# A three-stage network on one core: weight decoding in written order, down products three column blocks behind

## The chip, the cores and the metric

One NeuronCore of a Trainium2 chip runs the whole program. The metric is the time of one execution on the device in microseconds (us); lower is better. TensorE is called PE in the views of the profile (its weight loads PEld), VectorE DVE, ScalarE ACT, GpSimd POOL and SyncE SP.

## The reference

Three stages follow one another on 4 sequences of 768 positions and 384 channels (8 heads of 48). All arrays are 32-bit; the weights of the last two stages come in as 64-bit floats, two words for a number.

```python
# 1. linear attention with decay, per batch and head
cur = u * k_t  (outer)  v_t
y_t = r_t @ (state + cur)
state = w * state + k_t (outer) v_t
# 2. gated feed-forward with a convolution over the sequence (384 -> 1024 -> 384)
h = relu(x @ w_in)
c = conv_w[0]*h[t-1] + conv_w[1]*h[t] + conv_w[2]*h[t+1]     # zeros beyond the ends
x = (h * sigmoid(c)) @ w_out
# 3. normalisation and feed-forward with a residual (384 -> 1536 -> 384)
xn = (x - mean) / sqrt(var + 1e-6) * g_ln
out = x + relu(xn @ w_ch1) @ w_ch2
```

## The kernel before

**Blocks and passes.** The 3072 positions are cut into 24 tiles of 128 for the attention and into 8 blocks of 384 (three tiles) for the two feed-forward stages. There are two passes over the blocks. The first (`mixer1`, blocks j = 0 to 7) does the convolution stage and spills its result to DRAM; the attention tiles are computed beside it. The second (`mixer2`) loads a block back, normalises it and does the last stage. The first four attention tiles come before block 0, in the loop `while finished[0] < EARLY - 1`.

**Products in three parts.** A 32-bit product is made of three products of a reduced 32-bit type: every operand is split into a high part and the remainder (`xh` and `xl`, `wih` and `wil`, `gh` and `gl`), and high x high, high x low and low x high are added in PSUM. So one column block f (128 hidden columns) of a block of positions takes nine products upward (`mm3`, into `psm`) and nine downward (`down`, into the three accumulators `acc`).

**A column block of the first pass.** `moe1_up` issues the nine upward products of column f, then the gate of column f - 1 (`gate`: sigmoid on ScalarE, product on VectorE), then relu, scaling (L371, L372, ScalarE) and two taps (L374, VectorE) of column f, then the split of the gated column f - 1 into `gh` (L360, ScalarE) and `gl` (L361, VectorE). The downward products are put into a list by `queue_down` and run by `pump`: with LAG = 2, column f - 2 goes down in the turn of column f. LAG also sets the number of `gh` and `gl` buffers, LAG + 1. After the upward and after the downward products of a turn, `after1` is called: 16 slots to a block. A slot takes one attention step and some decode steps.

**Attention steps.** `attn_tile` is a generator with five parts: transposes of r and k (`prt`, `pkt`) and the diagonal `aT`; state update (`pst`, `sn`, `sbds`) and the next tile's `kk`; products `dps` and masked copies into `aT`; an empty part; output products `yps`, their split into `xh` and `xl`, the loads of tile n + 3, and the copies of the one column that neighbouring blocks share (L320, L321). Block j of the first pass may begin when tile (j + 1) x 3 - (j mod 2) is done (the last one for j = 7), because of that shared column. Block 0 has 14 attention steps in its slots, the others 16.

**Weight decoding.** `wjob` makes a job of every slice of weights: jobs 0 to 2 (first half of w_in, 512 numbers a partition), 3 (w_out), 4 to 6 (second half of w_in), 7 to 9 (w_out), 10 to 15 (w_ch1), 16 to 21 (w_ch2), 768 numbers each where nothing else is said. A job is loaded into one of three `st` buffers. Its steps: absolute value of the high word (L111, ScalarE) and clamp (L112); shift (L114); two steps that put in the low word's bits and the sign (L117, L119) with the high copy (L140, ScalarE); the remainder (L143, for w_ch1 scaled by `g_ln`, L145). Four calls of the generator make a job, as the last step comes in one call with the next job's first. `wdo(n, last)` makes n such calls, up to job `last`, and loads a job ahead; `need(job)` makes as many calls as it takes to end that job.

**What sets the order.** The program text is an order for the planner of the framework: it simulates a time line and sets every engine's instructions in a fixed order, moving what is free to where its simulated engine has room. Steps given to `tc.keep_in_program_order` keep their written place among one another. Before, these were all TensorE instructions, the loads of `st` and `x1b`, and the two reductions of `choose_path`; the decode steps on VectorE and ScalarE were free.

Of the kernel before, what the change touches and what calls it, by code (L numbers as in the profile page):

```python
# [8 lines left out]
F32 = mybir.dt.float32  # L9
# [20 lines left out]
NP = H // 2  # L30
PR = 112
WN = 768
LAG = 2
EARLY = 4
GC = 16
GE = 4
# [7 lines left out]
def body(ctx, tc, r, k, v, w, u, w_in, conv_w, w_out, g_ln, w_ch1, w_ch2, out):  # L44
    nc = tc.nc
# [17 lines left out]
    class InOrder:  # L63


        def matmul(self, *args, **kw):
            return tc.keep_in_program_order(nc.tensor.matmul(*args, **kw))  # L67

        def transpose(self, *args, **kw):
            return tc.keep_in_program_order(nc.tensor.transpose(*args, **kw))  # L70

    pe = InOrder()


    ident = const.tile([128, 128], F32, name="ident")
# [29 lines left out]
    def decode(st, n):  # L105

        words = st[:, 0:2 * n].rearrange("p (n two) -> p n two", two=2)
        lo, hi = words[:, :, 0], words[:, :, 1]
        t = ap.tile([128, WN], F32, tag="wd", name="wdec", bufs=2)[:, 0:n]
        ti = t.bitcast(I32)  # L110
        a_.activation(out=t, in_=hi.bitcast(F32), func=AF.Abs)  # L111
        v_.tensor_scalar(out=t, in0=t, scalar1=W_MIN, scalar2=W_MAX, op0=ALU.max, op1=ALU.min)  # L112
        yield
        v_.tensor_scalar(out=ti, in0=ti, scalar1=5, scalar2=2, op0=ALU.logical_shift_left,  # L114
                         op1=ALU.logical_shift_right)
        yield
        v_.scalar_tensor_tensor(out=ti, in0=lo, scalar=29, in1=ti, op0=ALU.logical_shift_right, op1=ALU.bitwise_or)  # L117
        yield
        v_.scalar_tensor_tensor(out=ti, in0=hi, scalar=-(2 ** 30), in1=ti, op0=ALU.bitwise_and, op1=ALU.bitwise_or)  # L119
        return t  # L120

    wjobs = []
# [1 line left out]
    def wjob(src, n, hi, lo, scale=None):  # L124

        st = []

        def load():
            st.append(io.tile([128, 2 * WN], I32, tag="st", name="st", bufs=3))
            dst = st[0][:, 0:2 * n]  # L130
            if len(src.shape) == 3:
                dst = dst.rearrange("p (a n) -> p a n", a=src.shape[1])
            tc.keep_in_program_order(nc.sync.dma_start(out=dst, in_=src.bitcast(I32)))

        def steps():
            t = yield from decode(st[0], n)
            if len(src.shape) == 3:
                t = t.rearrange("p (a n) -> p a n", a=src.shape[1])
            kw = {} if scale is None else {"scale": gl[:, scale:scale + 1]}
            a_.activation(out=hi, in_=t, func=AF.Copy, **kw)  # L140
            yield
            if scale is None:
                v_.tensor_tensor(out=lo, in0=t, in1=hi.bitcast(F32), op=ALU.subtract)  # L143
            else:
                v_.scalar_tensor_tensor(out=lo, in0=t, scalar=kw["scale"], in1=hi.bitcast(F32),  # L145
                                        op0=ALU.mult, op1=ALU.subtract)
        wjobs.append((load, steps()))
        return len(wjobs) - 1
# [35 lines left out]
    def wdo(count=1, last=None):  # L184

        for _ in range(count):
            while w_done[0] < (len(wjobs) if last is None else last + 1):
                wload(w_done[0] + 2)
                if next(wjobs[w_done[0]][1], "end") != "end":
                    break  # L190
                w_done[0] += 1
# [359 lines left out]
    def tables():  # L551
# [2 lines left out]
        wv = w.rearrange("(p two) d -> two d p", two=2)  # L554
        for q in range(2):
            nc.sync.dma_start(out=wc[64 * q:64 * q + D], in_=wv[q].unsqueeze(2), allow_slow_non_contiguous=True)
        load_tile(0)
        nc.sync.dma_start(out=tku[:, 1], in_=u.unsqueeze(0).to_broadcast([128, H, D]))
        wload(1)
        load_tile(1)  # L560
        wload(2)
# [49 lines left out]
    def conv_weights(cst):  # L611
        t = yield from decode(cst, 3 * NF1)
        v_.tensor_copy(out=cw, in_=t.rearrange("p (k f) -> p k f", k=3))

    def choose_path():

        wr = sp.tile([1, DM], F32, tag="wr", name="wr", bufs=1)
        ok = sp.tile([1, 4], F32, tag="ok", name="ok", bufs=1)
        nc.sync.dma_start(out=wr, in_=w.rearrange("h d -> (h d)").unsqueeze(0))
        tc.keep_in_program_order(v_.tensor_reduce(out=ok[:, 0:1], in_=wr, axis=AX.X, op=ALU.max))  # L620
        tc.keep_in_program_order(v_.tensor_reduce(out=ok[:, 1:2], in_=wr, axis=AX.X, op=ALU.min))
        v_.tensor_scalar(out=ok[:, 2:3], in0=ok[:, 0:1], scalar1=DECAY_MAX, scalar2=None, op0=ALU.is_le)
        v_.tensor_scalar(out=ok[:, 3:4], in0=ok[:, 1:2], scalar1=DECAY_MIN, scalar2=None, op0=ALU.is_ge)
        v_.tensor_tensor(out=ok[:, 0:1], in0=ok[:, 2:3], in1=ok[:, 3:4], op=ALU.mult)
        v_.tensor_scalar(out=general, in0=ok[:, 0:1], scalar1=0.5, scalar2=None, op0=ALU.is_lt)
# [27 lines left out]

    cst = tables()
    decayed_k(0)
    for _ in conv_weights(cst):
        pass
    tau, early = 0, {}
    while finished[0] < EARLY - 1:
        if tau % 3 == 0 and tau // 3 < EARLY:  # L660
            early[tau // 3] = attn_tile(tau // 3)
        for gen in early.values():
            next(gen, None)
        wdo(1 + tau % 2)
        tau += 1
    ahead = [iter(())]
    for j in range(NB):
        slot = [0]
        while finished[0] < min((j + 1) * TT - (j % 2), NT - 1):
            step()  # L670

        def before1(f):
            if f < NF1:
                need(wi_job[f // 4])
            if f >= LAG:
                need(wo_job[min(f - LAG + 1, NF1 - 1)])

        def after1(f):
            if j or f:
                step()  # L680
            slot[0] += 1
            if j == 0:
                wdo(2)
            elif j < NB - 2:
                wdo(slot[0] % 2, c1_job[NF2 - 1])
            else:
                wdo(1, c2_job[4])
            if j == NB - 1:
                if slot[0] == 1:
                    ahead[0] = prefetch(0)  # L690
                elif slot[0] % 4 == 0:
                    next(ahead[0], None)

        mixer1(xT[j], spill(j), before1, after1)
# [3 lines left out]
    for j in range(NB):  # L698
        def before2(f):
            need(c1_job[f])  # L700
            need(c2_job[f])

        def after2(f):
            wdo(2)
            if f == 1 and j + 1 < NB:
                ahead[0] = prefetch(j + 1)
            if f >= 4:
                next(ahead[0], None)

        b, s0 = divmod(j, BPB)  # L710
        x1s, xn = normed.pop(j)
        mixer2(xn, lambda acc, x1s=x1s, b=b, s0=s0: finish(
            acc, x1s, lambda t0: out[b, s0 * T + t0:s0 * T + t0 + 128, :]), before2, after2)
    pump(0)
    flag = nc.values_load(general[0:1, 0:1], min_val=0, max_val=1)
    with tc.If(flag != 0):
# [31 lines left out]
```

## Time and profile before

| | us |
|---|---|
| time, median of 3 runs (707.03 to 709.63) | 708.38 |
| the profiled execution's own time | 709.03 |
| its span, first to last instruction | 707.5 |
| TensorE busy | 650.5 |
| VectorE busy | 434.9 |
| ScalarE busy | 271.4 |
| GpSimd busy | 98.8 |

Busy times overlap between engines and do not add up to the span. Ends of products are modelled, so TensorE that is busy throughout is not TensorE at its peak. Where an engine idles, the views name what ended the wait. The mean granted clock of TensorE over the span was 0.965 of its full 2.4 GHz.

### The profile page before, as it was taken

How to read it: one execution, taken by the hardware profiler on the slowest of the kernel's cores; microseconds unless marked ns; L12 is line 12 of the kernel's file. 1: busy time of each engine (PE TensorE's matmuls, PEld its weight loads, DVE VectorE, ACT ScalarE, POOL GpSimd, SP SyncE). 2: the span in 40 equal slices, each digit the busy share in tenths (PEclk: the TensorE clock that was granted, in tenths of full speed). 3: DMA queues.
4: the chain of work that ended last, by engine and by line, in shares of the span. 5: the costliest groups of instructions: out<-in, count | busy, mean ns of one | idle time of the engine just before them, and what ended most of it. 6: DMA issues, size and time to landing. Idle time of an engine off the chain costs nothing.

```text
span 707.5 us, 12380 instructions
## 1 busy us (share of the span) xinstructions
PE 650.5 (92%) x5100; PEld 615.1 (87%) x5100; DVE 434.9 (61%) x823; ACT 271.4 (38%) x537; POOL 98.8 (14%) x136
## 2 busy tenths in 40 slices
PE   4765888979999999999499999999999999999996
PEld 3655777869998999989498999999999999999996
DVE  5989999988788878797967534224241424242211
ACT  2436546655565655556566321212111111212110
POOL 5341211122113121230100000000000000000000
PEclk9976889999999999999799999999999999999999
DMA  8954452423132232305000302020010202020001
GB/s 147 228 153 112 124 169 68 120 49 92 34 91 45 58 79 45 103 2 198 4 35 1 112 1 67 1 68 1 29 39 1 68 1 68 0 68 1 34 1 38
DMA packets 93841, 45.14 MB, mean 64 GB/s; under 512 B 80337, under 2 KB 89682, under 8 KB 93778
## 3 DMA queue, kind: packets, MB, share of 16 engines
q1 hardware_dynamic: 93778, 44.28, 23.7%
q8 instruction: 42, 0.69, 0.4%
q14 instruction: 21, 0.17, 0.1%
HBM read 34.83 MB, written 9.44 MB: 63 GB/s over the span
## 4 chain that ended last, share of the span: by engine, by line
PE 71%; DVE 18%; DMA 4%; issue 2%; ACT 2%; SPq 2%; POOL 1%; ACTq 0%; DVEq 0%; POOLq 0%
PE acc L67 32%; PE psm L67 31%; DVE c L374 3%; PE yps L67 3%; DMA st<-in_moe_w_ch_dram 2%; PE dps L67 2%; DVE aT L287 2%; DVE wdec L117 2%; DVE wdec L119 1%; DVE wdec L112 1%; DVE gl L361 1%; PE pxt L70 1%; DVE kk L222 1%; DVE c L355 1%; DVE wdec L114 1%
## 5 line engine op out<-in xcount | busy, mean ns | idle before, releaser
L388 DVE SCALAR_TENSOR_TENSOR rl<-psm,rh 128x384 fp32r<-128x384 f32 x96 | 53.4, 556 | 146.8 <-ACT rh L387 146.8
L387 ACT ACTIVATE rh<-psm 128x384 fp32r<-128x384 f32 x96 | 47.3, 493 | 216.5 <-PE psm L67 213.9
L67 PE MATMUL psm<-xnh,c1h 128*128 128x384 f32 x288 | 99.1, 344 | 0.6 <-ACT xnh L331 0.6
L67 PE MATMUL psm<-xnl,c1h 128*128 128x384 f32 x288 | 97.5, 339 | 0.8 <-DVE xnl L332 0.8
L67 PE MATMUL psm<-xnh,c1l 128*128 128x384 f32 x288 | 97.6, 339 | 0.0
L67 PE MATMUL acc<-c2l,rh 128*128 128x384 f32 x288 | 97.1, 337 | 0.0
L67 PE MATMUL acc<-c2h,rl 128*128 128x384 f32 x288 | 97.1, 337 | 0.0
L67 PE MATMUL acc<-c2h,rh 128*128 128x384 f32 x288 | 97.0, 337 | 0.0
L374 DVE SCALAR_TENSOR_TENSOR c<-h,cw,c 128x384 f32<-128x384 f32 x128 | 86.5, 677 | 11.1 <-ACT c L372 10.0
L67 PE MATMUL acc<-woh,gh 128*128 128x384 f32 x192 | 70.5, 367 | 11.6 <-ACT gh L360 11.6
L67 PE MATMUL acc<-woh,gl 128*128 128x384 f32 x192 | 68.4, 356 | 12.5 <-DVE gl L361 12.5
L67 PE MATMUL psm<-xh,wih 128*128 128x386 f32 x192 | 72.3, 377 | 4.9 <-POOL xl L316 4.6
L67 PE MATMUL psm<-xl,wih 128*128 128x386 f32 x192 | 67.8, 353 | 2.4 <-POOL xl L320 2.4
L67 PE MATMUL psm<-xh,wil 128*128 128x386 f32 x192 | 67.0, 349 | 0.0
L67 PE MATMUL acc<-wol,gh 128*128 128x384 f32 x192 | 66.8, 348 | 0.0
L411 POOL TENSOR_TENSOR rs<-rs,nhalf 128x1 f32<-128x1 f32 x24 | 14.4, 615 | 304.3 <-DVE rs L410 304.1
L354 ACT ACTIVATE c<-c 128x384 f32<-128x384 f32 x64 | 33.5, 524 | 59.4 <-DVE c L374 59.4
L67 PEld LDWEIGHTS psm<-xnl,c1h 128*128 128x128 f32 x288 | 54.4, 189 | 1.1 <-DVE xnl L332 1.0
L67 PEld LDWEIGHTS psm<-xnh,c1h 128*128 128x128 f32 x288 | 54.4, 189 | 0.9 <-ACT xnh L331 0.9
L254 POOL TENSOR_TENSOR av<-kk,rvbuf 128x384 f32<-128x384 f32 x24 | 33.4, 1390 | 155.3 <-DVE kk L222 129.2
L67 PEld LDWEIGHTS psm<-xnh,c1l 128*128 128x128 f32 x288 | 54.2, 188 | 0.0
L67 PEld LDWEIGHTS acc<-c2h,rh 128*128 128x128 f32 x288 | 54.1, 188 | 0.0
(108 smaller groups left out, 1175.7 us busy)
## 6 DMA issues: line engine op xcount, KB each, us to landing
st<-in_moe_w_ch_dram SPq DMA_DIRECT2D x12, 768.0 KB, 5.8
rvbuf<-in_r_dram SPq DMA_DIRECT2D x24, 192.0 KB, 3.2
kt<-in_k_dram SPq DMA_DIRECT2D x24, 192.0 KB, 3.2
rvbuf<-in_v_dram SPq DMA_DIRECT2D x24, 192.0 KB, 2.9
x_dram<-x SPq DMA_DIRECT2D x24, 192.0 KB, 2.0
x1b<-x_dram SPq DMA_DIRECT2D x24, 192.0 KB, 2.8
out_dram<-x1b SPq DMA_DIRECT2D x24, 192.0 KB, 1.9
st<-in_moe_w_in_dram SPq DMA_DIRECT2D x6, 512.0 KB, 5.1
```

The source lines that it names most:

```text
L67: return tc.keep_in_program_order(nc.tensor.matmul(*args, **kw))
L70: return tc.keep_in_program_order(nc.tensor.transpose(*args, **kw))
L112: v_.tensor_scalar(out=t, in0=t, scalar1=W_MIN, scalar2=W_MAX, op0=ALU.max, op1=ALU.min)
L114: v_.tensor_scalar(out=ti, in0=ti, scalar1=5, scalar2=2, op0=ALU.logical_shift_left, op1=ALU.logical_shift_right)
L117: v_.scalar_tensor_tensor(out=ti, in0=lo, scalar=29, in1=ti, op0=ALU.logical_shift_right, op1=ALU.bitwise_or)
L254: g_.tensor_tensor(out=av, in0=kk[:, 1, :, 0:D], in1=rt[:, :, 0:D], op=ALU.mult)
L287: v_.copy_predicated(out=aT[:, q], mask=later.bitcast(I32), data=dps[q])
L354: a_.activation(out=st["c"], in_=st["c"], func=AF.Sigmoid)
L374: v_.scalar_tensor_tensor(out=c, in0=h[:, o:o + T], scalar=cw[:, tap, f:f + 1], in1=c, op0=ALU.mult, op1=ALU.add)
L387: a_.activation(out=gh, in_=ps[:, 0:T], func=AF.Relu)
L388: v_.scalar_tensor_tensor(out=gl_, in0=ps[:, 0:T], scalar=0.0, in1=gh.bitcast(F32), op0=ALU.max, op1=ALU.subtract)
L411: g_.tensor_tensor(out=rs[:, 1:2], in0=rs[:, 0:1], in1=nhalf, op=ALU.pow)
```

## The change

The decode steps on VectorE and ScalarE, and the loads, go through wrappers that keep the written order (`vo`, `ao`, `so`); all other work of these engines stays free. The spread of the decode calls over the slots changes: before block 0 only the first half of w_in may be decoded; in block 0 no further than the last w_out job; in blocks 1 to 5 every third slot takes a call instead of every second; in blocks 6 and 7 every second slot instead of each. The conv weights' decode moves behind the early attention tiles. LAG becomes 3: the downward products run three column blocks behind, in both passes, `gh` and `gl` have four buffers, and the weights for them are needed a column later. In block 1, the second one, three slots take one more attention step. The prefetch of the second pass's first block is advanced in every slot from the seventh on instead of every fourth, and what is left of a prefetch is drained after every block of the second pass. The load of `u` is written before the loads of tile 0.

```diff
-LAG = 2
+LAG = 3
...
-    pe = InOrder()
+        def __init__(self, engine):
+            self.engine = engine
+
+        def __getattr__(self, name):
+            op = getattr(self.engine, name)
+            return lambda *args, **kw: tc.keep_in_program_order(op(*args, **kw))
+
+    pe = InOrder(nc.tensor)
+    vo = InOrder(nc.vector)
+    ao = InOrder(nc.scalar)
+    so = InOrder(nc.sync)
...
-        a_.activation(out=t, in_=hi.bitcast(F32), func=AF.Abs)
-        v_.tensor_scalar(out=t, in0=t, scalar1=W_MIN, scalar2=W_MAX, op0=ALU.max, op1=ALU.min)
+        ao.activation(out=t, in_=hi.bitcast(F32), func=AF.Abs)
+        vo.tensor_scalar(out=t, in0=t, scalar1=W_MIN, scalar2=W_MAX, op0=ALU.max, op1=ALU.min)
...
-            a_.activation(out=hi, in_=t, func=AF.Copy, **kw)
+            ao.activation(out=hi, in_=t, func=AF.Copy, **kw)
             yield
             if scale is None:
-                v_.tensor_tensor(out=lo, in0=t, in1=hi.bitcast(F32), op=ALU.subtract)
+                vo.tensor_tensor(out=lo, in0=t, in1=hi.bitcast(F32), op=ALU.subtract)
...
+        nc.sync.dma_start(out=tku[:, 1], in_=u.unsqueeze(0).to_broadcast([128, H, D]))
         load_tile(0)
-        nc.sync.dma_start(out=tku[:, 1], in_=u.unsqueeze(0).to_broadcast([128, H, D]))
...
-    for _ in conv_weights(cst):
-        pass
     tau, early = 0, {}
...
-        wdo(1 + tau % 2)
+        wdo(1 + (tau % 4 == 3), wi_job[0])
         tau += 1
+    for _ in conv_weights(cst):
+        pass
...
-            if f >= LAG:
-                need(wo_job[min(f - LAG + 1, NF1 - 1)])
+            if f >= LAG - 1:
+                need(wo_job[f - LAG + 1])
...
         def after1(f):
+            slot[0] += 1
             if j or f:
                 step()
-            slot[0] += 1
+            if j == 1 and slot[0] in (4, 8, 12):
+                step()
             if j == 0:
-                wdo(2)
+                wdo(2, wo_job[NF1 - 1])
             elif j < NB - 2:
-                wdo(slot[0] % 2, c1_job[NF2 - 1])
+                wdo(slot[0] % 3 == 0, c1_job[NF2 - 1])
             else:
-                wdo(1, c2_job[4])
+                wdo(slot[0] % 2 == 0, c2_job[4])
             if j == NB - 1:
                 if slot[0] == 1:
                     ahead[0] = prefetch(0)
-                elif slot[0] % 4 == 0:
+                elif slot[0] >= 7:
                     next(ahead[0], None)
...
             need(c1_job[f])
-            need(c2_job[f])
+            need(c2_job[max(f - LAG + 1, 0)])
...
-            if f >= 4:
+            elif f >= 4:
                 next(ahead[0], None)
...
+        for _ in ahead[0]:
+            pass
```

## Rows read from the trace of the kernel before

**Rows 1.** The page of the profile: busy time of each engine with its share of the span and its instructions, and the busy tenths of TensorE and VectorE in 40 equal slices of 17.7 us.

```profile
PE 650.5 (92%) x5100; PEld 615.1 (87%) x5100; DVE 434.9 (61%) x823; ACT 271.4 (38%) x537; POOL 98.8 (14%) x136
...
PE   4765888979999999999499999999999999999996
...
DVE  5989999988788878797967534224241424242211
```

**Rows 2.** Busy time by stretch of the span: from and to, length, busy time and instructions of PE, PEld, DVE, ACT and POOL, mean granted clock, DMA share, GB/s. The first stretch lies before block 0; the next seven are blocks 0 to 3, 5, 6 and 7 of the first pass, each from its first product to that of the next block; the last two are the first two blocks of the second pass.

```profile
0.00:47.81 47.81, 26.87 (x364) 21.22 (x365) 40.56 (x90) 16.18 (x31) 23.28 (x52) 0.95 0.82 173
47.81:103.58 55.77, 43.63 (x343) 38.75 (x343) 51.59 (x84) 31.24 (x54) 9.21 (x6) 0.78 0.50 147
103.58:152.73 49.15, 44.20 (x466) 38.58 (x465) 48.48 (x81) 29.29 (x57) 12.24 (x14) 0.95 0.33 83
152.73:196.18 43.45, 41.09 (x401) 37.53 (x401) 33.43 (x56) 22.54 (x46) 9.11 (x9) 0.96 0.27 59
196.18:236.25 40.07, 40.07 (x452) 36.28 (x449) 33.88 (x59) 23.34 (x49) 8.78 (x12) 1.00 0.30 65
...
275.85:315.93 40.08, 40.03 (x435) 36.27 (x434) 33.78 (x61) 23.68 (x49) 11.62 (x12) 1.00 0.19 50
315.93:359.26 43.33, 34.34 (x281) 31.89 (x281) 34.47 (x66) 23.00 (x44) 4.05 (x4) 0.88 0.23 83
359.26:386.45 27.19, 26.55 (x154) 25.94 (x154) 19.62 (x37) 18.36 (x39) 0.00 (x0) 1.00 0.06 23
386.45:426.46 40.01, 39.23 (x226) 38.87 (x226) 18.67 (x43) 11.54 (x22) 1.65 (x3) 1.00 0.15 50
426.46:465.26 38.80, 38.80 (x227) 38.69 (x227) 12.98 (x30) 7.40 (x15) 1.65 (x3) 1.00 0.09 31
```

**Rows 3.** The time line before block 0 (and one row of block 0): start, duration, engine, line, operation, out<-in, number of instructions, and the idle time before the first with what ended it.

```profile
15.37 1.10 PE L70 MATMUL prt<-ident,rvbuf 128*112 128x128 f32 x4
...
20.65 2.44 PE L67 MATMUL yps<-aT,rvbuf 128*32 128x128 f32 x32 [3.33 <-DVE aT L287]
...
42.56 0.41 PE L67 MATMUL yps<-aT,rvbuf 128*32 128x128 f32 x4 [3.68 <-DVE aT L287]
...
43.98 0.84 ACT L140 ACTIVATE woh<-wdec 128x768 fp32r<-128x768 f32 x1 [1.34 <-DVE wdec L119]
...
46.51 0.63 ACT L140 ACTIVATE wih<-wdec 128x512 fp32r<-128x512 f32 x1
...
74.89 0.60 PE L70 MATMUL prt<-ident,rvbuf 128*112 128x128 f32 x4
```

**Rows 4.** Groups of VectorE's instructions up to 103.58 us, shapes kept apart: line, operation, names and shapes, count | busy us, mean ns | idle time before.

```profile
L119 DVE SCALAR_TENSOR_TENSOR wdec<-st,wdec 128x768 int32<-128x768 int32 x6 | 5.7, 947 | 0.0
L117 DVE SCALAR_TENSOR_TENSOR wdec<-st,wdec 128x768 int32<-128x768 int32 x6 | 5.7, 946 | 0.0
...
L114 DVE TENSOR_SCALAR wdec<-wdec 128x768 int32<-128x768 int32 x7 | 4.8, 680 | 0.0
...
L112 DVE TENSOR_SCALAR wdec<-wdec 128x768 f32<-128x768 f32 x7 | 4.1, 591 | 0.0
L117 DVE SCALAR_TENSOR_TENSOR wdec<-st,wdec 128x512 int32<-128x512 int32 x6 | 4.1, 686 | 0.1
L143 DVE TENSOR_TENSOR wil<-wdec,wih 128x512 fp32r<-128x512 f32 x6 | 4.1, 682 | 0.0
L119 DVE SCALAR_TENSOR_TENSOR wdec<-st,wdec 128x512 int32<-128x512 int32 x6 | 4.1, 682 | 0.0
L114 DVE TENSOR_SCALAR wdec<-wdec 128x512 int32<-128x512 int32 x6 | 4.0, 665 | 0.0
L143 DVE TENSOR_TENSOR wol<-wdec,woh 128x768 fp32r<-128x768 f32 x4 | 3.8, 951 | 0.0
...
L112 DVE TENSOR_SCALAR wdec<-wdec 128x512 f32<-128x512 f32 x6 | 3.0, 492 | 2.3 <-ACT wdec L111 2.3
```

**Rows 5.** The time line of TensorE in blocks 0, 2 and 6 and at the start of the second pass: products with idle time before them (columns as in rows 3).

```profile
62.24 0.69 PE L67 MATMUL acc<-woh,gh 128*128 128x384 f32 x1 [3.94 <-ACT gh L360]
...
152.73 0.44 PE L67 MATMUL psm<-xh,wih 128*128 128x386 f32 x1 [1.68 <-POOL xl L316]
155.53 0.44 PE L67 MATMUL psm<-xl,wih 128*128 128x386 f32 x1 [2.36 <-POOL xl L320]
...
347.30 0.69 PE L67 MATMUL acc<-woh,gh 128*128 128x384 f32 x1 [6.55 <-ACT gh L360]
...
386.45 0.44 PE L67 MATMUL psm<-xnh,c1h 128*128 128x384 f32 x1 [0.64 <-ACT xnh L331]
...
387.67 0.45 PE L67 MATMUL psm<-xnl,c1h 128*128 128x384 f32 x1 [0.78 <-DVE xnl L332]
```

**Rows 6.** Groups of VectorE's instructions in block 3 (196.18 to 236.25 us): the gate work.

```profile
L374 DVE SCALAR_TENSOR_TENSOR c<-h,cw,c 128x384 f32<-128x384 f32 x17 | 11.7, 690 | 1.1 <-ACT c L372 0.8
L361 DVE TENSOR_TENSOR gl<-c,gh 128x384 fp32r<-128x384 f32 x8 | 4.4, 556 | 2.1 <-ACT gh L360 1.8
L355 DVE TENSOR_TENSOR c<-h,c 128x384 f32<-128x384 f32 x8 | 4.4, 552 | 1.9 <-ACT c L354 1.8
```

**Rows 7.** One group of VectorE's instructions in block 6 (315.93 to 359.26 us): the last mask step of the decoding.

```profile
L119 DVE SCALAR_TENSOR_TENSOR wdec<-st,wdec 128x768 int32<-128x768 int32 x3 | 2.9, 955 | 0.0
```

**Rows 8.** Who waited for whom over the span: VectorE's clamp for ScalarE's absolute value. Total us, times, longest.

```profile
DVE wdec L112 <- ACT wdec L111: 6.8, 6, 2.3
```

More of the change, by code (lines that the diff above doesn't have):

```diff
@@ L63, in body @@
     class InOrder:
[L66 to L70, printed above, removed]
-    pe = InOrder()
+        def __init__(self, engine):
[7 more added lines that the diff above has]
+    so = InOrder(nc.sync)
     ident = const.tile([128, 128], F32, name="ident")
@@ L110, in decode @@
         ti = t.bitcast(I32)
-        a_.activation(out=t, in_=hi.bitcast(F32), func=AF.Abs)
-        v_.tensor_scalar(out=t, in0=t, scalar1=W_MIN, scalar2=W_MAX, op0=ALU.max, op1=ALU.min)
+        ao.activation(out=t, in_=hi.bitcast(F32), func=AF.Abs)
+        vo.tensor_scalar(out=t, in0=t, scalar1=W_MIN, scalar2=W_MAX, op0=ALU.max, op1=ALU.min)
         yield
-        v_.tensor_scalar(out=ti, in0=ti, scalar1=5, scalar2=2, op0=ALU.logical_shift_left,
+        vo.tensor_scalar(out=ti, in0=ti, scalar1=5, scalar2=2, op0=ALU.logical_shift_left,
                          op1=ALU.logical_shift_right)
         yield
-        v_.scalar_tensor_tensor(out=ti, in0=lo, scalar=29, in1=ti, op0=ALU.logical_shift_right, op1=ALU.bitwise_or)
+        vo.scalar_tensor_tensor(out=ti, in0=lo, scalar=29, in1=ti, op0=ALU.logical_shift_right, op1=ALU.bitwise_or)
         yield
-        v_.scalar_tensor_tensor(out=ti, in0=hi, scalar=-(2 ** 30), in1=ti, op0=ALU.bitwise_and, op1=ALU.bitwise_or)
+        vo.scalar_tensor_tensor(out=ti, in0=hi, scalar=-(2 ** 30), in1=ti, op0=ALU.bitwise_and, op1=ALU.bitwise_or)
         return t
@@ L132, in load @@
                 dst = dst.rearrange("p (a n) -> p a n", a=src.shape[1])
-            tc.keep_in_program_order(nc.sync.dma_start(out=dst, in_=src.bitcast(I32)))
+            so.dma_start(out=dst, in_=src.bitcast(I32))
         def steps():
@@ L139, in steps @@
             kw = {} if scale is None else {"scale": gl[:, scale:scale + 1]}
-            a_.activation(out=hi, in_=t, func=AF.Copy, **kw)
+            ao.activation(out=hi, in_=t, func=AF.Copy, **kw)
             yield
             if scale is None:
-                v_.tensor_tensor(out=lo, in0=t, in1=hi.bitcast(F32), op=ALU.subtract)
+                vo.tensor_tensor(out=lo, in0=t, in1=hi.bitcast(F32), op=ALU.subtract)
             else:
-                v_.scalar_tensor_tensor(out=lo, in0=t, scalar=kw["scale"], in1=hi.bitcast(F32),
+                vo.scalar_tensor_tensor(out=lo, in0=t, scalar=kw["scale"], in1=hi.bitcast(F32),
                                         op0=ALU.mult, op1=ALU.subtract)
@@ L619, in choose_path @@
         nc.sync.dma_start(out=wr, in_=w.rearrange("h d -> (h d)").unsqueeze(0))
-        tc.keep_in_program_order(v_.tensor_reduce(out=ok[:, 0:1], in_=wr, axis=AX.X, op=ALU.max))
-        tc.keep_in_program_order(v_.tensor_reduce(out=ok[:, 1:2], in_=wr, axis=AX.X, op=ALU.min))
+        vo.tensor_reduce(out=ok[:, 0:1], in_=wr, axis=AX.X, op=ALU.max)
+        vo.tensor_reduce(out=ok[:, 1:2], in_=wr, axis=AX.X, op=ALU.min)
         v_.tensor_scalar(out=ok[:, 2:3], in0=ok[:, 0:1], scalar1=DECAY_MAX, scalar2=None, op0=ALU.is_le)
```

## The prediction

> **What bounds the kernel now.** I read the page first. Over the whole span TensorE is the busiest engine, with 92% busy time, and VectorE has 61% [rows 1]. These are averages over stages with different limits. The slices show it: VectorE stands at 8 to 9 tenths up to about slice 9 (some 160 us), then at 7, and from slice 20 on at 2 to 4; TensorE is full in almost every slice after the tenth, with one dip near slice 20 [rows 1].
>
> So I cut the span at the first product of every block: the stretch before the first block, blocks 0 to 7 of the first pass, and the second pass. Busy time by stage [rows 2] gives three kinds. In the 105 us of blocks 0 and 1, VectorE is busy 51.6 of 55.8 us and 48.5 of 49.2 us: it is the bound, and TensorE waits for it. In blocks 3 to 5 TensorE is busy without a hole (40.1 of 40.1 us) and VectorE has 33.8 us: TensorE is the bound. Block 6 fits neither: 43.3 us with TensorE at 34.3 and VectorE at 34.5 busy. The second pass is TensorE's alone.
>
> The idle time in front of single products says who is late [rows 5]. In block 0, `acc` products wait 3.94 us for `gh`; at the start of block 2, the first two products wait 1.68 and 2.36 us for the columns of `xh` and `xl`; in block 6 an `acc` product waits 6.55 us for `gh`; at the start of the second pass 0.64 and 0.78 us go to `xnh` and `xnl`. All of these are VectorE's or ScalarE's results coming late. In the stretch with the long waits the clock is at its half level for part of the time: block 0 has a mean of 0.78 of full clock and block 6 has 0.88, so about 24.5 and 10.4 us of them ran at 1.2 GHz instead of 2.4 (twice the missing share, times the stage).
>
> **The change part by part.** *Decoding out of blocks 0 and 1.* Up to 103.58 us VectorE decoded the 10 jobs that the first block needs, two w_ch1 jobs and the beginning of a third. From the groups of that stretch [rows 4], a 512-wide job costs 0.69 + 0.68 + 0.68 + 0.67 + 0.49 = 3.2 us of VectorE and a 768-wide job 0.95 + 0.95 + 0.68 + 0.59 + 0.95 = 4.1 us. The ten rows add up to 43.4 us; with the scaled last step of two w_ch1 jobs and the conv weights (estimated from the same widths: 2 us and 1.4 us) it is 46.8 us. After the change block 0 may not go past the last w_out job: 6 jobs of 3.2, 4 of 4.1 and 1.4 make 37.1 us (unrounded), 9.7 us less.
>
> The stretch before block 0 will be shorter but will use VectorE worse, because it may now decode three jobs only. Today two of its waits are for `aT`, 3.33 and 3.68 us [rows 3], on an engine that is busy 40.6 of 47.8 us [rows 2]; the fourth and fifth job end in it (their `woh` and `wih` copies run at 43.98 and 46.51 us [rows 3]). Without those jobs I expect both waits to go, so block 0 begins near 47.8 - 7.0 = 40.8 us. VectorE loses about 4.1 + 3.2 + half a job, 9 us of work, in it: 31.5 busy of 40.8, idle 9.3 instead of 7.2, so 2.1 us of VectorE time is wasted. Between "none wasted" and "all 7 us wasted" I take 2.1, because the tile-by-tile chain remains the limit there: the four transposes of a tile still take 1.10 us at the low clock against 0.60 later [rows 3].
>
> Block 0 stays VectorE's. Its end is today's 103.58, less 9.7 of decoding, plus 2.1 idle, less 2.6 because the third column block of delay lets one more column's gate work be outstanding at the end (11.7 + 4.4 + 4.4 us for eight columns [rows 6], 2.6 each): 93.4; I take 94.4 for the decoding burst that `need` forces ahead of column 4. Ends: 88 (waste none, idle of block 0 halved and the burst free) and 100 (all decoding as stretched as the slowest row).
>
> *Block 1* loses the rest of the w_ch1 decoding and gets five decode steps (slots 3, 6, 9, 12, 15) and three more attention steps. VectorE: 33.9 as in block 3, which has no decoding and the same 16 attention steps [rows 2]; 4.9 for the decode steps (a job's 4.1, 0.2 for the scaled last step by estimate, and the next job's first 0.6); 2.5 for three fifths of a tile, at (33.9 - 20.5)/3.2 = 4.2 us a tile: 41.3. TensorE: a product comes every 0.175 us (a block of the second pass, 216 products and nine transposes, takes 38.8 us [rows 2]); 8 columns of 18 make 25.2, a tile (40.1 - 25.2)/3.2 = 4.7, three fifths 2.8: 42.9. TensorE is late by a little, 43.5 us, where it was 49.2. The extra steps bring the loads of a later tile (three DMAs) and two POOL operations forward too; POOL is 12.2 of 49.2 us busy and DMA 0.33 [rows 2], which covers them.
>
> *Block 2* began with 1.68 + 2.36 us of waiting, as 14 + 16 steps end tile 9 exactly on the last step before it. Three steps more give the halo three slots of lead. It becomes a block like 3, plus half a microsecond: 40.5 instead of 43.45.
>
> *Blocks 3 to 5* get five decode steps each (4.9 us of VectorE): 33.8 + 4.9 = 38.7 against TensorE's 40.1. That is 97%. Block 1 of today shows VectorE at 48.5 of 49.2, 99% [rows 2], so it can be that full; I add 1.0 us for all three, since the gate work has a column more to come late in, and keep +2 each as the upper end (the 92.5% of block 0). What is added here is a wait in front of gate work: behind a decode step that waits for ScalarE stand the gates on VectorE's queue, and for their `gl` the `acc` product three columns on.
>
> *Block 6* loses the hoisted decoding: three jobs ran there (three executions of the last mask step [rows 7]), 12.3 us, beside the norms of the first tiles. Now it holds eight decode steps, two jobs, 8.2 us, and three attention steps fewer. VectorE: 34.5 - 12.3 + 8.2 - 2.5 = 27.9. TensorE: 34.3 less half of the 10.4 us at half clock, less 2.8: 26.3. So 27.9, and 29.0 with some friction, instead of 43.3. This is the largest single term. *Block 7* takes one job: VectorE 19.6 + 4.1 = 23.7 under TensorE's 27.2, no change. The earlier prefetch steps end the last split long before the second pass, so 0.64 + 0.78 = 1.4 us go. The extra column of delay moves nine products past each block boundary and back at the end: 9 x 0.175 = 1.6 us to add once. The accumulators of a block are emptied a column later, but the next block's first `acc` product also comes a column later.
>
> Edits at nothing: the `u` load goes ahead of tile 0's loads (0.6 us on SP's queue, under the table chain that the first transposes wait for); the conv weights move on the same engine, within the same stage; the later need of w_ch2 and the drain of `ahead` lie in the second pass, where VectorE is busy 18.7 of 40.0 us [rows 2].
>
> **The sum.** Second pass begins at 94.4 + 43.5 + 40.5 + 120.75 + 29.0 + 27.2 = 355.4 instead of 386.45: 31.1 less. Less 1.4, plus 1.6: 30.9. The profiled span is 707.5 in an execution of 709.03 (1.5 around it), so 676.6 and 678.1 us. The median of the runs is 708.38, 0.65 under the profiled one, which is no more than their scatter; I forecast 678.
>
> **A rule beside the rows.** Block 0 ran 24.5 us at half clock, while VectorE was busy 92.5% of it [rows 2]: I give its return no price. The Trainium skill, "TensorE: Matmul & The Clock Gate", section Terms, prices throttled time at that time by the missing share, which would be 12 us here. By that rule these 12 us come on top, 666 us, on the side of the fourth rival; VectorE's share in that row speaks against it.
>
> **The rivals.**
> 1. *VectorE stays the bound through block 6* (0.22). At 97% any step written in order that finds ScalarE late leaves VectorE standing. 2 us for each of blocks 1 to 5, 3 us in block 0 and 2 in block 6 make 15: 693. For: today it waited 6.8 us for `Abs` results in six places [rows 8]. Against: block 1 at 99%.
> 2. *Slower* (0.06). A decode job hands over twice to ScalarE and back (`Abs`, then the high copy). Pinned, job after job, the next `Abs` stands behind the last copy. If VectorE's queue finds nothing to put into both holes, a job costs two ScalarE passes (0.84 us a copy [rows 3]) and what is queued ahead of them, 3 us. It counts in jobs 3 to 15, 13 jobs that lie where VectorE is full: 39 us, and 678 + 39 = 717. It decides from 31/13 = 2.4 us per job on. The longest such wait in the trace is 2.3 us, in one place [rows 8]; gate work and attention work stay free to fill the holes, so I rate it low.
> 3. *The order hardly changes* (0.06): the planner sets pinned steps where the free ones stood, the caps do little, and only the delay and the extra steps tell: the 4 us of block 2, some 4 of block 0: 700.
> 4. *TensorE becomes the bound already in block 0* (0.14): block 1 begins at 88, 42.8, 40, 119.75, 28, 27.2: 345.8, 40.5 less in all: 668.
>
> **Chances.** Forecast 0.52 (about 671 to 687 with its own bounds), rivals 0.22, 0.06, 0.06, 0.14. The range 666 to 696 leaves out the two small rivals and the outer parts of 1 and 4, somewhat under 0.2. Faster by over 0.3% (2.1 us, about what a measurement of this kernel can tell) is everything but rival 2 and the weak end of 3: 0.93; within 0.3% 0.01; slower 0.06.
>
> **What would show it.** In the changed profile: block 0 begins near 41 and block 1 near 94 us; VectorE is busy 90% or more of block 0, and some 38 to 39 us of each of blocks 2 to 5; no wait of a first product of block 2 for `xl`; block 6 under 30 us, with no `acc` product waiting over 2 us for `gh` and the clock at its full level; 38.8 us for the second pass's first block. The forecast is wrong if block 0 ends after 100, if blocks 2 to 5 grow over 42 us each with `acc` waiting for `gl`, or if `wdec` steps have waits for ScalarE of 2 us and more in front of them throughout.

## The result and the profile after

The changed kernel takes 686.03 us (median of 4 runs, 685.23 to 686.52) against 708.62 us before (4 runs): a ratio of 0.968, 95% interval 0.966 to 0.970, faster by 22.6 us. 678 was forecast, with a range from 666 to 696: the direction and the range hold, the gain is about three quarters of the 30.9 us that were worked out.

The profiled execution (685.23 us, span 683.5) by stages, cut at the same products as in [rows 2]; the columns are from and to, length, busy time of PE, PEld, DVE, ACT, POOL, granted clock, DMA share, GB/s. The first row lies before block 0, the next eight are blocks 0 to 7 of the first pass, the last two the first and last block of the second pass.

```profile
0.00:41.88 41.88, 26.05 (x364) 20.36 (x364) 33.74 (x74) 12.62 (x26) 20.46 (x51) 0.96 0.87 165
41.88:97.16 55.28, 40.95 (x333) 34.94 (x334) 48.54 (x84) 29.01 (x51) 6.06 (x5) 0.81 0.41 113
97.16:142.78 45.62, 44.46 (x505) 38.98 (x505) 42.24 (x72) 26.90 (x55) 13.98 (x17) 1.00 0.42 102
142.78:182.40 39.62, 38.66 (x395) 35.23 (x393) 35.99 (x62) 24.75 (x50) 9.07 (x10) 1.00 0.35 85
182.40:224.20 41.80, 41.42 (x489) 37.25 (x488) 37.12 (x66) 23.83 (x49) 10.84 (x13) 1.00 0.32 77
224.20:263.67 39.47, 39.30 (x405) 35.80 (x401) 36.53 (x62) 23.54 (x50) 8.19 (x8) 1.00 0.39 90
263.67:303.81 40.14, 39.93 (x432) 36.19 (x433) 37.83 (x64) 24.90 (x51) 10.04 (x10) 1.00 0.20 62
303.81:333.13 29.32, 28.82 (x217) 27.69 (x217) 23.53 (x49) 19.07 (x37) 3.17 (x3) 1.00 0.28 95
333.13:361.85 28.72, 26.86 (x155) 26.10 (x155) 27.60 (x57) 19.57 (x41) 2.06 (x3) 1.00 0.20 69
361.85:400.59 38.74, 38.74 (x226) 38.64 (x226) 23.49 (x43) 16.04 (x30) 0.00 (x0) 1.00 0.11 37
633.70:683.50 49.80, 42.74 (x244) 42.41 (x243) 9.68 (x18) 5.90 (x12) 0.00 (x0) 0.97 0.08 26
```

Set beside the forecast for each term:

| stage | before | forecast | after |
|---|---|---|---|
| block 0 begins | 47.8 | 40.8 | 41.9 |
| block 0 ends | 103.6 | 94.4 | 97.2 |
| block 1 | 49.2 | 43.5 | 45.6 |
| block 2 | 43.5 | 40.5 | 39.6 |
| blocks 3 to 5 | 119.8 | 120.8 | 121.4 |
| block 6 | 43.3 | 29.0 | 29.3 |
| block 7 | 27.2 | 27.2 | 28.7 |
| second pass begins | 386.5 | 355.4 | 361.9 |

From block 2 on every stage came within 2 us of its forecast; the second pass takes 321.6 us, 321.2 by the forecast's terms. Blocks 0 and 1 make up 4.9 of the 6.4 us that are missing at the start of the second pass. Block 0 itself has hardly shrunk (55.8 to 55.3 us); it only begins and ends earlier. VectorE is busy 48.5 of its 55.3 us, 88%, with 6.7 us of holes.

Where TensorE still waits, its time line shows (columns as in rows 3):

```profile
58.99 0.45 PE L71 MATMUL acc<-woh,gh 128*128 128x384 f32 x1 [2.04 <-ACT woh L71]
61.80 0.69 PE L71 MATMUL acc<-wol,gh 128*128 128x384 f32 x1 [2.37 <-DVE wol L71]
...
71.95 0.69 PE L71 MATMUL psm<-xh,wih 128*128 128x386 f32 x1 [4.23 <-ACT wih L71]
75.69 0.69 PE L71 MATMUL psm<-xh,wih 128*128 128x386 f32 x1 [2.22 <-ACT wih L71]
...
92.62 0.44 PE L71 MATMUL psm<-xh,wih 128*128 128x386 f32 x1 [1.68 <-DVE xl L316]
...
354.20 0.45 PE L71 MATMUL acc<-woh,gl 128*128 128x384 f32 x1 [1.86 <-DVE gl L365]
```

(Lines have moved by four; the wrappers' instructions all stand under L71.) The waits for `gh` [rows 5] and for `gl` are gone from block 0, and in their place stand four for weights: `woh` and `wol` of job 3, and `wih` of jobs 5 and 6 in front of column 4. One more, of 1.68 us in front of column 7, is put down to `xl`. Nothing waits any more at the start of block 2 or of the second pass.

### The profile page after: what moved, and what is told of

Same layout as the page of the kernel before. It is cut to its first block, busy times and chain, and to the rows that moved or that the text cites. A ratio compares the mean times of both kernels' runs of the same rounds, so it can differ in the third digit from the quotient of the medians.

```text
span 683.5 us, 12393 instructions
## 1 busy us (share of the span) xinstructions
PE 641.0 (94%) x5100; PEld 606.1 (89%) x5100; DVE 434.4 (64%) x823; ACT 270.4 (40%) x537; POOL 93.8 (14%) x136
## 4 chain that ended last, share of the span: by engine, by line
PE 69%; DVE 19%; ACT 2%; issue 2%; DMA 1%; POOL 0%; SPq 0%; DVEq 0%
PE psm L71 31%; PE acc L71 31%; DVE c L378 4%; DVE wdec L71 4%; PE yps L71 2%; DVE aT L291 2%; DVE gl L365 2%; PE dps L71 2%; DVE c L359 1%; PE pxt L71 1%; DVE kk L226 1%; PE pst L71 1%; PE pkt L71 1%; DMA x1b<-x_dram 1%; DVE sn L276 1%
## 5 line engine op out<-in xcount | busy, mean ns | idle before, releaser
L71 PE MATMUL psm<-xnh,c1h 128*128 128x384 f32 x288 | 99.0, 344 | 0.0
L71 PE MATMUL psm<-xnh,c1l 128*128 128x384 f32 x288 | 97.5, 339 | 0.0
L71 PE MATMUL acc<-c2h,rl 128*128 128x384 f32 x288 | 97.3, 338 | 0.0
L71 PE MATMUL acc<-c2h,rh 128*128 128x384 f32 x288 | 97.2, 338 | 0.0
L71 PE MATMUL acc<-c2l,rh 128*128 128x384 f32 x288 | 97.1, 337 | 0.0
L71 PE MATMUL psm<-xnl,c1h 128*128 128x384 f32 x288 | 97.0, 337 | 0.0
L71 PE MATMUL psm<-xh,wih 128*128 128x386 f32 x192 | 70.6, 368 | 11.6 <-ACT wih L71 6.5
L71 PE MATMUL acc<-woh,gh 128*128 128x384 f32 x192 | 69.6, 363 | 2.0 <-ACT woh L71 2.0
L71 PE MATMUL acc<-woh,gl 128*128 128x384 f32 x192 | 66.2, 345 | 2.4 <-DVE gl L365 2.4
L71 PE MATMUL acc<-wol,gh 128*128 128x384 f32 x192 | 65.9, 343 | 2.4 <-DVE wol L71 2.4
L71 PE MATMUL psm<-xl,wih 128*128 128x386 f32 x192 | 66.4, 346 | 0.2 <-POOL xl L324 0.2
L71 PE MATMUL psm<-xh,wil 128*128 128x386 f32 x192 | 66.3, 346 | 0.0
L71 PEld LDWEIGHTS psm<-xnl,c1h 128*128 128x128 f32 x288 | 54.4, 189 | 0.0
L71 PEld LDWEIGHTS psm<-xnh,c1h 128*128 128x128 f32 x288 | 54.4, 189 | 0.0
L71 PEld LDWEIGHTS psm<-xnh,c1l 128*128 128x128 f32 x288 | 54.2, 188 | 0.0
L71 PEld LDWEIGHTS acc<-c2l,rh 128*128 128x128 f32 x288 | 54.2, 188 | 0.0
L71 PEld LDWEIGHTS acc<-c2h,rh 128*128 128x128 f32 x288 | 54.1, 188 | 0.0
L71 PEld LDWEIGHTS acc<-c2h,rl 128*128 128x128 f32 x288 | 54.1, 188 | 0.0
```

The source lines that it names most:

```text
L71: return lambda *args, **kw: tc.keep_in_program_order(op(*args, **kw))
```

## The experiments

Every kernel ran beside runs of the kernel before on the same chip; ratios are to those, with 95% intervals.

**1. The pin alone.** The decode steps go through the pinning wrappers; the small edits (`u` load, the later need of w_ch2, the drain) stay, all else is as before.

```diff
-LAG = 3
+LAG = 2
...
-        wdo(1 + (tau % 4 == 3), wi_job[0])
+        wdo(1 + tau % 2)
...
-                wdo(2, wo_job[NF1 - 1])
+                wdo(2)
...
-                wdo(slot[0] % 3 == 0, c1_job[NF2 - 1])
+                wdo(slot[0] % 2, c1_job[NF2 - 1])
...
-            if j == 1 and slot[0] in (4, 8, 12):
-                step()
```

(and the conv weights' place, blocks 6 and 7 and the prefetch likewise as before)

> The kernel before with the decode steps pinned in written order, the old spread of the decode calls, two column blocks of delay, no extra attention steps. Theory A (the gain is decoding work taken out of stretches where VectorE is full; the pin alone does not take it out of block 0, where the old calls still ask for 8 jobs): block 0 stays at 55 to 58 us, block 1 falls to some 45 because less decoding is left over for it, block 6 to some 36; 696 to 702 us in all. Theory B (the written order itself brings the gain, the spread little): 686 to 692 us.

Measured: 704.11 us, 0.992 (0.989 to 0.995).

```profile
0.00:44.23 44.23, 25.63 (x364) 19.97 (x364) 33.23 (x80) 13.10 (x27) 21.60 (x51) 0.92 0.82 171
44.23:99.79 55.56, 42.41 (x342) 37.81 (x343) 51.09 (x83) 29.98 (x53) 8.98 (x6) 0.79 0.50 136
316.05:356.12 40.07, 34.74 (x281) 32.28 (x281) 32.69 (x63) 22.38 (x43) 3.18 (x4) 0.91 0.27 90
```

These are the stretch before block 0, block 0 and block 6. The pin starts block 0 3.6 us earlier (decode steps no longer go ahead of the first tiles' work: VectorE has 33.2 us in that stretch instead of 40.6) and takes 3.3 us off block 6. Block 0 stays as long as it was. In all it brings some 5 us. That is 2 us above theory A's range: block 1 (53.4 us, where 45 were expected) and block 6 (40.1, not 36) are longer than it said. Block 1 does have a little less decoding, as theory A said (17.2 us of VectorE's time against 18.8 before), but more gate work (22.4 against 19.9 us), so it is longer than before (49.2 us) all the same. Theory B is out.

**2 to 4. The spread and the delay, each undone and both.** All three keep the pin, the extra attention steps and the earlier prefetch. Run 2 has the old spread with a delay of three, run 3 the new spread with a delay of two, run 4 the old spread with two.

```diff
# runs 2 and 4
-        wdo(1 + (tau % 4 == 3), wi_job[0])
+        wdo(1 + tau % 2)
...
-                wdo(2, wo_job[NF1 - 1])
+                wdo(2)
...
-                wdo(slot[0] % 3 == 0, c1_job[NF2 - 1])
+                wdo(slot[0] % 2, c1_job[NF2 - 1])
...
-                wdo(slot[0] % 2 == 0, c2_job[4])
+                wdo(1, c2_job[4])
# runs 3 and 4
-LAG = 3
+LAG = 2
```

> The changed kernel with the old spread of the decode calls (before block 0, in block 0, in blocks 1 to 5 and in blocks 6 and 7); pin, three column blocks of delay and extra attention steps stay. Theory A: 692 to 698 us, block 0 longer by some 5 us for the w_ch1 jobs in it, block 6 above 32. Theory B: 685 to 689 us.

> The changed kernel with a delay of two column blocks instead of three. Theory A: 688 to 692 us, with the loss in blocks 0, 6 and 7, where acc products wait for gh and gl again. Theory C (the delay is the main thing, because the waits for gh and gl were the waits of TensorE): over 697 us.

> The changed kernel with both the old spread and a delay of two; pin, extra attention steps and earlier prefetch stay. Theory A: 694 to 700 us, the losses of the two runs before about added. Theory B: under 692 us. Theory C: over 700 us and no further than 2 us from the run with the new spread and a delay of two.

| | delay two | delay three |
|---|---|---|
| old spread | 699.64 us, 0.987 (0.984 to 0.989) | 695.05 us, 0.979 (0.977 to 0.982) |
| new spread | 687.21 us, 0.968 (0.966 to 0.971) | 686.03 us, 0.968 (0.966 to 0.970) |

The spread brings 9.0 us at a delay of three (about 8 by the ratios) and 12.4 at two. The delay brings 4.6 us with the old spread and nothing that can be told apart with the new one: 1.2 us, 0.2%. So theory C is out, and so is the thought that the waits for `gh` and `gl` asked for more delay: they were the sign of a VectorE that was overfull, and with the decoding spread they are mostly gone without it (in run 3 none over 0.5 us in block 0, 1.14 and 0.99 us in block 6). Run 3 is 0.8 us under theory A's range. Its profiled execution, 2.5 us above the median, has longer stages where theory A put them (block 0 at 61.6 us, block 6 at 32.1, of which 1.6 us in each direction are only the column that moves past the block boundary), but in block 0 the products wait for weights and not for `gh` and `gl`. Run 4 lies in theory A's range, though its loss of 13.6 us is more than those of runs 2 and 3 added (9.0 and 1.2).

Where the old spread costs is in block 1 of run 2, and it shows as VectorE without a hole; after the change the same block had 42.2 of 45.6:

```profile
42.14:94.76 52.62, 40.24 (x334) 34.97 (x334) 46.45 (x82) 27.54 (x52) 8.21 (x6) 0.82 0.42 117
94.76:147.23 52.47, 46.19 (x506) 39.15 (x505) 52.47 (x89) 32.23 (x61) 20.41 (x16) 1.00 0.48 129
338.18:371.97 33.79, 29.54 (x155) 28.78 (x155) 27.20 (x58) 20.31 (x42) 4.88 (x5) 0.90 0.05 18
```

Block 2 is 2.9 us longer too (42.5 against 39.6). Against the expectation, block 0 of run 2 is 2.7 us shorter than after the change (first row). The old spread writes five jobs before it, but only three end there, as after the change; block 0 has 22.7 us of decoding instead of 25.9 because the end of the w_out decoding slid into block 1. And block 6 stays short (28.7 us); block 7 is the longer one (third row, 33.8). That led to runs 6, 10 and 11.

**5. Mask steps left out.** Jobs 3 to 9 go without the steps that put in the low word's bits and the sign, so their weights lack them.

```diff
         yield
-        vo.scalar_tensor_tensor(out=ti, in0=lo, scalar=29, in1=ti, op0=ALU.logical_shift_right, op1=ALU.bitwise_or)
+        if masks:
+            vo.scalar_tensor_tensor(out=ti, in0=lo, scalar=29, in1=ti, op0=ALU.logical_shift_right, op1=ALU.bitwise_or)
         yield
-        vo.scalar_tensor_tensor(out=ti, in0=hi, scalar=-(2 ** 30), in1=ti, op0=ALU.bitwise_and, op1=ALU.bitwise_or)
+        if masks:
+            vo.scalar_tensor_tensor(out=ti, in0=hi, scalar=-(2 ** 30), in1=ti, op0=ALU.bitwise_and, op1=ALU.bitwise_or)
...
+        masks = not 3 <= len(wjobs) <= 9
```

> The changed kernel with the two mask steps (low word's bits, sign) of jobs 3 to 9 left out: the weights of the first pass come out with wrong bits, 11.7 us of VectorE's work fall away in block 0, no product or transfer does. Theory A (block 0 is still bound by VectorE's work): block 0 shrinks from 55.3 us by 8 to 11.7, the time falls to 674 to 678 us. Rival D (block 0 is bound by its chain: each decode job's hand-overs between ScalarE and VectorE and the order around them): less than 4 us.

Measured: 678.15 us, 0.957 (0.955 to 0.959): 7.9 us less than the changed kernel. Block 0, and TensorE's waits in the middle of it:

```profile
41.71:90.64 48.93, 38.85 (x334) 33.57 (x335) 40.01 (x74) 29.63 (x54) 8.91 (x7) 0.83 0.47 131
```

```profile
62.32 0.46 PE L71 MATMUL psm<-xh,wil 128*128 128x386 f32 x1 [1.51 <-DVE wil L71]
65.53 0.69 PE L71 MATMUL psm<-xh,wih 128*128 128x386 f32 x1 [2.76 <-ACT wih L71]
67.77 0.69 PE L71 MATMUL psm<-xh,wil 128*128 128x386 f32 x1 [1.23 <-DVE wil L71]
70.12 0.69 PE L71 MATMUL psm<-xh,wih 128*128 128x386 f32 x1 [1.66 <-ACT wih L71]
```

Of 11.7 us of VectorE's work 7.9 come out of the time: block 0 is bound by VectorE's work for the greater part. Theory A named more: the time is just above its 674 to 678 us, and block 0 is 6.4 us shorter, not 8 to 11.7, with VectorE idle for 8.9 us of it instead of 6.7. The four rows, 7.2 us for `wih` and `wil`, are the chain of jobs 4 to 6 through ScalarE and VectorE, which is left when there is less work to fill it; rival D has the smaller part.

**6. Job 3 before block 0.**

```diff
-        wdo(1 + (tau % 4 == 3), wi_job[0])
+        wdo(1 + (tau % 4 == 3), wo_job[0])
```

> The changed kernel with the decode calls before block 0 allowed one job further (job 3, the first of w_out), so that the 8 us in which VectorE stands idle before block 0 take 4.1 us of its work out of block 0. Theory A: block 0 begins up to 1 us later and is 3 to 5 us shorter, 682 to 684 us. Rival: the tile chain before block 0 is lengthened by as much: 686, no change.

Measured: 683.01 us, 0.963 (0.961 to 0.965). The time is in theory A's range. Block 0 begins at 41.36 us, no later, and ends at 94.75 instead of 97.16; but it is 1.9 us shorter, not 3 to 5, and not because job 3 went under idle time before it. VectorE's decode steps alone, before block 0, in it and in block 1 (from and to, length, busy time, clock, DMA share, GB/s), and TensorE's wait in front of column 4:

```profile
0.00:41.36 41.36, 11.69 (x16) 0.96 0.91 177
41.36:94.75 53.39, 22.89 (x38) 0.81 0.40 109
94.75:141.49 46.74, 5.89 (x7) 1.00 0.41 100
```

```profile
72.08 0.69 PE L71 MATMUL psm<-xh,wih 128*128 128x386 f32 x1 [6.70 <-ACT wih L71]
```

After the change the three stretches have 11.61, 25.86 and 3.98 us. So nearly all of job 3 still runs in block 0, in the hole at its start. TensorE waits longer in front of column 4 (6.70 us instead of 4.23) and is through with this wait and the next at the same time, 75.71 us against 75.69. What block 0 has less of is the end of the last w_out job, which slid into block 1. VectorE is idle for 6.7 us of block 0 in both. At the start of block 2 the profiled execution is 1.3 us ahead; where the rest of the 3.0 us between the medians lies stays open.

**7. w_out asked for a column later.**

```diff
-            if f >= LAG - 1:
-                need(wo_job[f - LAG + 1])
+            if f >= LAG:
+                need(wo_job[f - LAG])
```

> The changed kernel with the weights of w_out asked for a column later (only for the column that goes down in the turn), so that job 7 need not be decoded ahead of the upward products of column 4. Theory A: the burst ahead of column 4 is short of the job that nobody waits for yet; TensorE's two waits for wih (4.2 and 2.2 us) do not shrink, since job 6 ends them, but what follows is less late: 684 to 686 us. If the whole burst held TensorE up: 682 or less.

Measured: 688.28 us, 0.971 (0.970 to 0.973): 2.3 us slower, against both expectations. The waits in front of column 4 are the same 4.23 and 2.22 us; the saved place is paid at the end of the block, where a product now waits for a job that used to be ready:

```profile
85.30 0.45 PE L71 MATMUL acc<-woh,gh 128*128 128x384 f32 x1 [2.28 <-ACT woh L71]
```

So asking for job 7 that early is not what makes the burst dear; asked for later, it leaves VectorE idle for 9.4 us of block 0 instead of 6.7. What the burst of the jobs before it costs by itself is not shown.

**8. Without the extra attention steps.**

```diff
-            if j == 1 and slot[0] in (4, 8, 12):
-                step()
```

> The changed kernel without the three extra attention steps in block 1. Theory A: the wait for the shared column at the start of block 2 is back (some 2 to 4 us, with part of the clock's lower level after it), block 1 is 2.8 us shorter and block 6 as much longer: 687.5 to 690 us. Rival: block 1, with less work, ends that much earlier and the wait is hidden: 686, no change.

Measured: 688.61 us, 0.971 (0.969 to 0.973): 2.6 us slower, as expected, but only in part for the reason given. Blocks 1, 2, 6 and 7:

```profile
98.19:139.74 41.55, 40.68 (x465) 36.62 (x465) 38.94 (x68) 26.23 (x52) 10.38 (x15) 1.00 0.41 101
139.74:180.18 40.44, 39.57 (x400) 35.95 (x401) 34.75 (x59) 23.20 (x47) 9.30 (x9) 1.00 0.35 84
302.19:337.64 35.45, 33.21 (x282) 31.26 (x281) 28.32 (x57) 19.65 (x39) 5.19 (x4) 0.95 0.32 118
337.64:367.81 30.17, 28.37 (x155) 27.62 (x154) 27.75 (x57) 20.55 (x43) 2.06 (x3) 0.94 0.06 20
```

```profile
139.74 0.44 PE L71 MATMUL psm<-xh,wih 128*128 128x386 f32 x1 [0.87 <-POOL xl L320]
141.05 0.44 PE L71 MATMUL psm<-xl,wih 128*128 128x386 f32 x1 [0.87 <-POOL xl L324]
```

The wait at the start of block 2 is back at 0.87 + 0.87 us, less than half of the 4.0 before. The profiled execution is 1.3 us above the median. Most of its difference is in blocks 6 and 7, 65.6 us together against 58.0: the three steps cost 4.1 us where they are put (block 1; 2.6 against the block 1 of run 9, 44.1 us) and save 7.6 where they are taken away, where run 8 also has a wait of 1.58 us for `gh` and stretches of low clock (0.95 and 0.94).

**9 to 11. More before block 0.** Run 9 is the changed kernel again; run 10 allows up to job 4, run 11 up to job 6, two calls a turn.

```diff
# run 10
+        wdo(1 + (tau % 2), wo_job[0] + 1)
# run 11
+        wdo(2, wi_job[1])
```

> The changed kernel once more, beside the next two on the same chip: 686 us, block 0 at 55 us.

> The changed kernel with up to job 4 decoded before block 0 (one or two calls a turn, 21 in all). Theory A (block 0 is bound by VectorE's work, and work put under its idle time before block 0 comes out of it): another 1 to 3 us below the 683.0 of the run with job 3, 680 to 682 us, block 0 beginning no later than 42.5 us. If the idle time before block 0 is used up: 683 to 685, block 0 begins later by what it is shorter.

> The changed kernel with all of w_in and the first job of w_out (up to job 6) decoded before block 0, two calls a turn: 13.7 us of VectorE's work, more than the 8 us it stands idle there. Theory A: block 0 begins 3 to 6 us later, has no wait for wih in column 4 and is 8 to 12 us shorter: 680 to 684 us. Rival (PE's work, not VectorE's, sets block 0 once the burst is gone): block 0 stays over 48 us and the time rises to 686 or more.

Measured: 685.91 us, 0.968 (0.966 to 0.971); 683.15 us, 0.964 (0.962 to 0.967); 679.44 us, 0.959 (0.956 to 0.961). Block 0 of run 9 is 56.8 us long, not 55. Run 11 is the fastest kernel here that decodes all bits, 6.5 us under run 9.

```profile
0.00:42.86 42.86, 25.42 (x365) 19.41 (x365) 35.70 (x77) 13.34 (x26) 22.02 (x51) 0.97 0.86 183
42.86:93.74 50.88, 38.55 (x333) 34.54 (x334) 46.84 (x83) 29.43 (x54) 7.77 (x6) 0.79 0.41 108
```

```profile
61.49 0.18 DVE L617 COPY cw<-wdec 128x24 f32<-128x24 f32 x1
61.70 0.61 ACT L376 ACTIVATE c<-h,cw 128x384 f32<-128x384 f32 x1 [1.10 <-DVE cw L617]
67.21 0.69 PE L71 MATMUL acc<-woh,gh 128*128 128x384 f32 x1 [9.09 <-ACT gh L364]
```

Its block 0 (second row) is 4.4 us shorter than after the change (6.0 than in run 9), less than the 8 to 12 expected, and begins only 1 us later; its time is just under theory A's 680 us. VectorE's busy time before block 0 rises by 2.0 us, not by the 13.7 that were written there: written early is not run early, and but for four steps of job 3 all of jobs 3 to 6 ran in block 0. What falls is VectorE's idle time up to the end of block 0, 11.2 us instead of 14.9 (15.7 in run 9). The wait of 9.09 us has a cause of its own. The decode of the conv weights is written behind these jobs and pinned as well, so `cw` is there at 61.7 us, and the taps and gates of all columns stand behind it (the three rows); after the change it is there at 43.2 us, before the first column's products are done. No run writes it ahead of the jobs.

Run 10 gained nothing over run 6, one job less: its time is 1 us above theory A's, and its block 0 begins 0.8 us later than that of run 6 (42.18 us) and is 0.8 us shorter, as the other expectation had it.

## Why the prediction was right, and where it was off

**What bounds each stage** held in the main: VectorE in block 0 (with the old spread in block 1 too), TensorE in blocks 1 to 5 after the change. Run 5 shows it for block 0 (two thirds of the work taken from VectorE comes out of the time), run 2 for block 1. VectorE's share of block 0, 88%, is under the 90% that the prediction had named as a sign. That the decoding in these stages is what makes it overfull, more than the delay, is shown by runs 2 to 4: the spread is worth 9 to 12 us, the pin (run 1) about 5, the delay 0 to 5, the extra steps 2.6; they do not add up. No run has the new spread without the pin, and none undoes the earlier prefetch or the conv weights' new place alone, so how much of the spread's worth needs the written order stays open.

**Block 6**, the largest single term, came out at 29.3 against 29.0, without a wait over 0.5 us for `gh` or `gl` and at the full clock. But the sum had VectorE as its bound, at 27.9 us, with TensorE at 26.3; in the run TensorE is busy 28.8 of the 29.3 us and VectorE 23.5. That the number fits so well is partly luck. **Blocks 2 to 5** came out 0.9 us under (block 2) and 0.7 us over (3 to 5 together; block 3 alone is 1.7 us longer than before); 36 to 38 us of VectorE's work, where 38 to 39 were forecast, fit under 39 to 42 of TensorE's. The first rival, VectorE as the bound throughout, is out.

**Block 0 was sized too short**, by 2.8 us at its end (4.4 in run 9). Up to that end VectorE's idle time rose from 11.4 to 14.9 us, near the 14.5 that follow from the sum (2.1 of waste and 1 for the burst on top of 11.4). Its busy time fell by 9.9 us, from 92.2 to 82.3, where the sum took off 9.7 for decoding and 2.6 for gate work, 12.3 in all. The term that failed is the 2.6: the third column of delay was to leave one more column's gate work undone at the block's end. The gate work on VectorE up to that end, before and after (columns as in run 6):

```profile
0.00:103.58 103.58, 16.73 (x27) 0.86 0.65 159
0.00:97.16 97.16, 16.33 (x26) 0.88 0.61 135
```

That is one instruction and 0.4 us less, and in run 9 there are again 27 with 16.8 us. The decoding alone shrank by 8.1 us (45.6 to 37.5): the rows that the prediction added up overlap a little, so that their sum is more than VectorE's time. The attention work done up to there made up for it, with 12 masked copies instead of 14.

The idle time lies elsewhere than the sum had it. Before block 0 it is 8.1 us, where 9.3 were forecast; in the block it is 6.7, where 4.2 were taken over from before and 1 was allowed for the burst. These rows say where:

```profile
43.01 0.18 DVE L617 COPY cw<-wdec 128x24 f32<-128x24 f32 x1
46.68 1.27 DVE L378 SCALAR_TENSOR_TENSOR c<-h,cw,c 128x384 f32<-128x384 f32 x2 [3.49 <-ACT c L376]
...
71.93 0.80 DVE L71 TENSOR_TENSOR wil<-wdec,wih 128x512 fp32r<-128x512 f32 x1 [0.70 <-ACT wih L71]
72.65 0.87 DVE L71 TENSOR_SCALAR wdec<-wdec 128x512 f32<-128x512 f32 x2
73.56 1.42 DVE L71 SCALAR_TENSOR_TENSOR wdec<-st,wdec 128x512 int32<-128x512 int32 x2
75.67 0.69 DVE L71 TENSOR_TENSOR wil<-wdec,wih 128x512 fp32r<-128x512 f32 x1 [0.69 <-ACT wih L71]
```

First, VectorE stands 3.5 us at the start of block 0, until the first column's product is there: job 3 is written behind it, and nothing else fills the hole. Run 6 fills it with job 3, but VectorE is then idle as long elsewhere in the block. Second, high copies on ScalarE make VectorE wait: 0.7 us for each of jobs 5 and 6 in these rows, 2.7 us for all seven jobs of the block. This is the mechanism of the second rival, at less than a third of the 2.4 us a job from which it would have decided. The last rows are also why TensorE waits 2.22 us in front of column 4: job 6 alone, on an otherwise empty VectorE, takes 3.7 us from one `wil` to the next, and the wait for `wih` ends with it.

**Block 1** was sized 2.1 us short (0.6 by run 9; blocks 0 and 1 together end within 0.2 us of each other in the two executions). TensorE, its bound, is busy 44.5 us (44.0 in run 9), where 42.9 were worked out. The extra steps were priced at 2.8 us; run 8 puts them between 2.6 and 4.1, so how much of this term is price and how much is scatter between executions stays open.

**Block 7** was to stay at 27.2 us; the wait of 1.86 us for `gl` at 354.20 makes it 28.7. VectorE has 27.6 us there, against 23.7 in the forecast: work that block 6 did not do (23.5 instead of 27.9) moved over. The two blocks together have 51.1 us, and 51.6 were forecast.

**The clock.** Block 0 still has a mean of 0.81 of full clock, so about 21 of its 55.3 us at 1.2 GHz, where 24.5 had been. The Trainium skill, "TensorE: Matmul & The Clock Gate", section Terms, would price that at half the time, by estimate 10 us; no run here shows that price by itself. Run 5 shows that 7.9 us go with VectorE's work while the mean clock of the block hardly rises, from 0.81 to 0.83. In block 6, where TensorE is the bound after the change, the low clock went with the waits, and its return was part of the term.

**A loose reading** changes nothing in the sum: VectorE stands at 7 to 9 tenths up to slice 20 of [rows 1] and at 4 or less only from slice 24 on.

## What to carry to other kernels

A wait on an engine's time line names the result that was late; whether to delay the consumer or to lighten the producer is told by the producer's busy share in that stage; here lightening left the delay nothing that could be measured. Background work is to be spread to stages where its engine has room. Writing it earlier is not enough to have it run earlier: the trace has to say where the steps ended up. A step moved out of a stage should be priced in both stages by their own rows.

## What the runs showed that was not expected

The pin is weaker than the account of the kernel ahead of the prediction says. ScalarE's time line in the changed kernel:

```profile
50.77 0.67 ACT L71 ACTIVATE wdec<-st 128x512 f32<-128x512 f32 x1
...
58.09 0.84 ACT L71 ACTIVATE woh<-wdec 128x768 fp32r<-128x768 f32 x1
```

The first is the absolute value of job 4, the second the high copy of job 3, which is written before it. So the pin does not keep all pinned steps of an engine in their written order, and the premise of the second rival, that the next job's first step must stand behind the last copy, did not hold for job 4. A reading that fits is that a pinned step only keeps behind what is written just before it on its engine; no run tests it. In the late part of the block (75.0 and 75.6 us) the written order and the order run do agree.
